# Float32 loads of q, k and V on SP's queue, with the casts moved onto the engines, in an attention and router kernel

## The chip, the cores and the metric

The kernel runs on one core of one Trainium2 chip. The metric is the device time of one execution in microseconds (us). The kernel before has a median of 495.98 us in three runs (494.5 to 497.27).

## What is computed

Two stages follow each other. The first is attention in chunks, for 4 batches, 8 heads, 768 positions and a head size of 64, with inputs in float32. Each chunk of 32 queries sees 16 positions to its left, its own 32, 8 to its right, and 8 memory rows of its head:

```python
for c in range(nc):                       # 24 chunks of 32
    l_start = max(0, c * 32 - 16)
    r_end = min(S, c * 32 + 32 + 8)
    k_full = np.concatenate([mem_k, k[:, :, l_start:r_end]], axis=2)
    v_full = np.concatenate([mem_v, v[:, :, l_start:r_end]], axis=2)
    scores = scale * np.matmul(q_c, k_full.transpose(0, 1, 3, 2))
    a = softmax(scores)
    out[:, :, c_start:c_end] = np.matmul(a, v_full)
```

Its output, 3072 tokens of 512 numbers, goes into a mixture of 8 experts with noisy top-2 routing: `noisy = x @ w_gate + log1p(exp(x @ w_noise)) * noise`. The two best experts of a token compute `relu(x @ w1[e]) @ w2[e]`, and the two results are added with softmax weights.

## The kernel before, in words

**Attention.** Head h and head h+4 are worked on together, in partitions 0 to 63 and 64 to 127; four such pairs make a batch, and the kernel counts 16 pairs n in all. For a pair, `qkT(n)` transposes q and k on PE (L328, L334) and copies them out of PSUM into `qT` (ACT, L330) and `kT` (DVE, L337). `kT` holds 24 windows of 64 columns each: 56 context columns, and 8 memory columns that POOL copies in from `mkT` (L338). `scores(n)` is 48 matmuls of 64 columns (L347), a maximum and a subtraction on DVE (L352, L354), and the exponential on ACT (L355). `probT(n)` transposes the probabilities (PE L362, ACT copy L364). `mix(n)` multiplies them with the windows of V (PE L379), divides by the sum that comes out as column 64 (DVE L383, L384) and writes a tile `xrow` for the batch.

**Loads.** `load_qk(b)` (L249) and `load_v(b)` (L268) are DMAs on POOL's queue that read float32 and write bf16. They read rows of 64 numbers, 256 bytes each: 12,288 rows for q and k of a batch and 10,752 for its V. V is laid out as windows, so that most positions are read twice. The memory rows of V go first into `mv_nat` (L302) and from there into the windows on SP's queue (L271). POOL then multiplies the first and last window by a mask (L274). q and k have two buffers, so batch b+2 is loaded when batch b is done, and so are the two window tiles `vwin0` and `vwin1`.

**Router.** `dispatch(b)` takes a batch's `xrow`, transposes it (L129), copies (L131, DVE and ACT in turn), computes the logits, picks the two experts with some forty small DVE instructions, counts ranks with PE (L169 to L191), and scatters the 6 x 128 rows with indirect DMAs of POOL (L223) into a DRAM table `x_by_pair`, one bucket of 128 rows for each of the 28 pairs of experts, and a spill area behind them. Before that, `fill_blank` writes empty rows to the whole table on SP's queue (L85).

**Experts.** After attention, SP reads the spill rows (L470) and bucket after bucket (L433); eight experts follow (PE L495, L530), their weights cast to bf16 by DMAs on POOL's queue (L420, L421), two experts ahead. A loop at the end (L554) handles spill rows past the first 32; it has no iteration on these inputs.

**Order.** Each engine runs its own instructions in order. The program's order is set by the loop below, and a scheduler moves instructions that do not depend on each other. Tiles come from pools; the pools of the experts are laid over the space that attention's pool `apool` gives back, so what lies on it waits for the end of attention.

```python
for n in range(NPAIR):
    if n + 2 < NPAIR: qkT(n + 2)
    probT(n)
    if n + 1 < NPAIR: scores(n + 1)
    mix(n)
    if n == 0: fill_blank()
    if hp == HP - 1 and b + 2 < B: load_qk(b + 2); load_v(b + 2)
    if hp == 0 and b > 0: dispatch(b - 1, xrows[b - 1])
dispatch(B - 1, xrows[B - 1])
```

Of the kernel before, what the change touches and what calls it, by code (L numbers as in the profile page):

```python
# [12 lines left out]
F32 = mybir.dt.float32  # L13
BF16 = mybir.dt.bfloat16
F32R = mybir.dt.float32r
AX = mybir.AxisListType.X
Alu = mybir.AluOpType
# [4 lines left out]
def kernel(  # L22
# [14 lines left out]
    nc = tc.nc  # L37
    B, H, S, D = q.shape
    n_mem = mem_k.shape[2]
    chunk, left_ctx, right_ctx = 32, 16, 8  # L40
    ncnk = S // chunk
# [13 lines left out]

    identb = const.tile([128, 128], BF16)
# [10 lines left out]
    NROW = NB * CAP + N + 128  # L67
# [13 lines left out]
    def fill_blank():  # L81
        blank = rcon.tile([128, ROW], I32, name="blank")
        nc.vector.memset(blank, 0)
        nc.vector.memset(blank[:, XC:XC + 1].bitcast(F32), float(PAD_TOK))
        nc.sync.dma_start(  # L85
            out=xd.rearrange("(g p) r -> p g r", p=128),
            in_=blank.rearrange("p (o r) -> p o r", o=1).to_broadcast([128, NROW // 128, ROW]),
        )
# [28 lines left out]
    n_spill_i = rcon.tile([128, 1], I32, name="n_spill_i")  # L117

# [3 lines left out]
    def dispatch(b, xrow):  # L122
# [3 lines left out]
        for t in range(BT):  # L126
            p_x = psT.tile([128, KP, 128], BF16, name="p_x", tag="tr")
            for kp in range(KP):
                nc.tensor.transpose(out=p_x[:, kp, :], in_=xrow[:, t, kp * 64:(kp + 1) * 64].bitcast(BF16), identity=identb)  # L129
            xt = rpool.tile([128, KP, 128], BF16, name="xt")  # L130
            (nc.scalar.copy if t % 2 else nc.vector.tensor_copy)(xt, p_x)  # L131
            for kp in range(KP):
                nc.tensor.matmul(out=ps_l[:, t, :], lhsT=xt[:, kp, :], rhs=wgn[:, kp, :], start=(kp == 0), stop=(kp == KP - 1))
# [92 lines left out]
        if b == B - 1:  # L226
            nc.tensor.matmul(out=ps_o[:, BT:BT + 1], lhsT=ones, rhs=seen_ov, start=True, stop=True, skip_group_check=True)
            nc.vector.tensor_scalar(out=n_spill_i, in0=ps_o[:, BT:BT + 1], scalar1=float(SPILL), scalar2=None, op0=Alu.max)
# [4 lines left out]
    psS = actx.enter_context(tc.psum_pool(name="psS", bufs=3))  # L233
    psT = actx.enter_context(tc.psum_pool(name="psT", bufs=2))
# [9 lines left out]
    def load_qk(b):  # L244
        qn = apool.tile([128, HP, BT, 2, D], BF16, name="qn")
        kn = apool.tile([128, HP, BT, 2, D], BF16, name="kn")
        for dst, src in ((qn, q), (kn, k)):
            for hh in range(2):
                nc.gpsimd.dma_start(out=dst[:, :, :, hh, :].rearrange("p h t d -> p (h t) d"),  # L249
                                    in_=src[b, HP * hh:HP * hh + HP].rearrange("h (t p) d -> p (h t) d", p=128))  # L250
        return qn, kn

    def load_v(b):
        vw = vwins[b % 2]
        for hh in range(2):
            p0 = 64 * hh
            o0 = v[b, HP * hh, 0].offset - left_ctx * D
            dst = vw[p0:p0 + WIN, :, :, 0:D].rearrange("p h c d -> p (h c) d")
            src = lambda c, n, j=0, nj=WIN: bass.AP(v.tensor, o0 + (c * chunk + j) * D, [[D, nj], [chunk * D, n], [1, D]])
            nch = HP * ncnk  # L260
            lo, hi = 0, nch
            if b == 0 and hh == 0:
                nc.gpsimd.dma_start(out=dst[left_ctx:, 0:1, :], in_=src(0, 1, left_ctx, WIN - left_ctx))
                lo = 1
            if b == B - 1 and hh == 1:
                nc.gpsimd.dma_start(out=dst[:WIN - right_ctx, nch - 1:nch, :], in_=src(nch - 1, 1, 0, WIN - right_ctx))
                hi = nch - 1
            nc.gpsimd.dma_start(out=dst[:, lo:hi, :], in_=src(lo, hi - lo))  # L268
            for hp in range(HP):
                h = HP * hh + hp  # L270
                nc.sync.dma_start(out=vw[p0 + WIN:p0 + CTX, hp, :, 0:D],  # L271
                                  in_=mv_nat[b * n_mem:(b + 1) * n_mem, h:h + 1, :].to_broadcast([n_mem, ncnk, D]))
        for c, col in ((0, live[:, 0:1]), (ncnk - 1, live[:, 1:2])):
            nc.gpsimd.tensor_scalar(out=vw[:, :, c, 0:D], in0=vw[:, :, c, 0:D], scalar1=col, scalar2=None, op0=Alu.mult)  # L274
# [15 lines left out]
    vwins = []  # L290
    for i in range(2):
        vw = const.tile([128, HP, ncnk, VW], BF16, name=f"vwin{i}")
        nc.gpsimd.memset(vw[:, :, 0, :], 0.0)
        nc.gpsimd.memset(vw[:, :, ncnk - 1, :], 0.0)
        vwins.append(vw)
    mk_nat = const.tile([B * n_mem, HP, 2, D], BF16, name="mk_nat")
    mv_nat = const.tile([B * n_mem, H, D], BF16, name="mv_nat")
    qk = {0: load_qk(0)}
    for b in range(B):
        for hh in range(2):  # L300
            nc.gpsimd.dma_start(out=mk_nat[b * n_mem:(b + 1) * n_mem, :, hh, :], in_=mem_k[b, HP * hh:HP * hh + HP].rearrange("h m d -> m h d"))
        nc.gpsimd.dma_start(out=mv_nat[b * n_mem:(b + 1) * n_mem], in_=mem_v[b].rearrange("h m d -> m h d"))  # L302

# [4 lines left out]

# [5 lines left out]
    p_m = psT.tile([128, HP, B * n_mem], BF16, name="p_m", tag="tr")  # L314
    for hp in range(HP):
        nc.tensor.transpose(out=p_m[:, hp, :], in_=mk_nat[:, hp, :, :], identity=identb[:B * n_mem, :B * n_mem])  # L316
# [5 lines left out]

    def qkT(n):
        b, hp = divmod(n, HP)
        qn, kn = qk[b]
        p_q = psT.tile([128, S], BF16, name="p_q", tag="tr")
        for t in range(BT):
            nc.tensor.transpose(out=p_q[:, t * 128:(t + 1) * 128], in_=qn[:, hp, t, :, :], identity=identb)  # L328
        qT = apool.tile([128, S], BF16, name="qT", bufs=3)
        nc.scalar.copy(qT, p_q)  # L330
        p_k = psT.tile([128, PADL + S + PADR], BF16, name="p_k", tag="tr")
        spots = [(0, 0), (BT - 1, PADL + S + PADR - 128)] + [(t, PADL + t * 128) for t in range(BT)]
        for t, o in spots:
            nc.tensor.transpose(out=p_k[:, o:o + 128], in_=kn[:, hp, t, :, :], identity=identb)  # L334
        kT = apool.tile([128, ncnk, CTX], BF16, name="kT", bufs=3)
        win = bass.AP(p_k.tensor, p_k.offset, [p_k.ap[0], [chunk, ncnk], [1, WIN]])
        nc.vector.tensor_copy(kT[:, :, :WIN], win)  # L337
        nc.gpsimd.tensor_copy(kT[:, :, WIN:], mkT[:, hp:hp + 1, b * n_mem:(b + 1) * n_mem].to_broadcast([128, ncnk, n_mem]))  # L338
        st[n].update(qT=qT, kT=kT)

    def scores(n):
        qT, kT = st[n]["qT"], st[n]["kT"]
        ps = [psS.tile([128, BT, CTX], F32, name="ps_s") for _ in range(2)]
        for c in range(ncnk):
            u, r = divmod(c, 4)
            for hh in range(2):
                nc.tensor.matmul(out=ps[hh][32 * r:32 * r + 32, u, :], lhsT=qT[64 * hh:64 * hh + 64, chunk * c:chunk * (c + 1)],  # L347
                                 rhs=kT[64 * hh:64 * hh + 64, c, :], start=True, stop=True)
        P = apool.tile([128, BT, 2, CTX], BF16, name="P")
        for hh in range(2):  # L350
            mx = apool.tile([128, BT], F32, name="mx", bufs=4)
            nc.vector.tensor_reduce(out=mx, in_=ps[hh], axis=AX, op=Alu.max)  # L352
            sd = apool.tile([128, BT, CTX], F32, name="sd", bufs=4)
            nc.vector.tensor_tensor(out=sd, in0=ps[hh], in1=mx.rearrange("p (u o) -> p u o", o=1).to_broadcast([128, BT, CTX]), op=Alu.subtract)  # L354
            nc.scalar.activation(out=P[:, :, hh, :], in_=sd, func=Act.Exp, scale=scale)  # L355
        st[n]["P"] = P

    def probT(n):
        P = st[n]["P"]
        p_p = psT.tile([128, BT, 128], BF16, name="p_p", tag="tr")  # L360
        for u in range(BT):
            nc.tensor.transpose(out=p_p[:, u, :], in_=P[:, u, :, :], identity=identb)  # L362
        PT = apool.tile([128, BT, 128], BF16, name="PT")
        nc.scalar.copy(PT, p_p)  # L364
        st[n]["PT"] = PT
# [187 lines left out]
    end = nc.values_load(n_spill_i[0:1, 0:1], min_val=SPILL, max_val=N)  # L553
    with tc.For_i(SPILL, end, 128) as i:  # L554
        xl = ld.tile([128, ROW], I32, name="xl")
        nc.sync.dma_start(out=xl, in_=xd[bass.ds(i + NB * CAP, 128), :])
# [3 lines left out]
        nc.vector.tensor_copy(lt, xl[:, XC:XC + 1].bitcast(F32))  # L560
# [7 lines left out]
        for e in range(E):  # L568
# [12 lines left out]
            in_=o, in_offset=None, bounds_check=N - 1, oob_is_err=False)  # L581

# [29 lines left out]
```

## Time and profile before

| what | number |
|---|---|
| median of the three runs | 495.98 us |
| the profiled execution's own time | 495.14 us |
| its span, which all times in the trace count from | 493.4 us |
| busy: PE, DVE, POOL, ACT | 300.5, 166.4, 140.9, 117.2 us |
| first scores L347, first mix L379 | 80.85, 85.77 us |
| last mix done (end of L384) | 218.33 us |
| first spill rows on PE (L476), first expert matmul (L495) | 243.71, 251.36 us |

The page's second part cuts the span into 40 slices of 12.3 us and gives busy shares in tenths; the list of waits says which engine stood idle at which line until what; the timeline gives a start, a duration, the engine, the line, and the idle time ahead in brackets with what ended it. The windows view gives, for a stretch of time, busy time and count of instructions by engine, the granted PE clock, the mean share of the DMA engines, and the GB/s that landed.

### The profile page before, as it was taken

Reading aid. Unit: us, or ns where it says so; the run is one execution under the profiler, and the core shown is the slowest. Engines: PE = TensorE matmul, PEld = TensorE weight load, DVE = VectorE, ACT = ScalarE, POOL = GpSimd, SP = SyncE. Lnnn points to the kernel's source line nnn. Section 1 sums busy time; section 2 is a strip of 40 time slices with the busy share of each in tenths; the row PEclk is TensorE's granted clock in tenths of the full one; section 3 lists DMA queues with packets and bytes.
Section 4 is the critical chain, followed back from the end, with each engine's and each line's share of the span. In section 5 each row is a group of like instructions: output and inputs, shape, how many; then the busy total and the mean of one; then the engine's idle time right before and its main releaser. Section 6 shows DMA issues by size and latency. Waiting matters only on the chain. (4 is left out here: it accounts for less than half of the span.)

```text
span 493.4 us, 8944 instructions
## 1 busy us (share of the span) xinstructions
PE 300.5 (61%) x3745; PEld 179.0 (36%) x3761; DVE 166.4 (34%) x474; ACT 117.2 (24%) x189; POOL 140.9 (29%) x220
## 2 busy tenths in 40 slices
PE   0002103475536246441089779689998999999991
PEld 0002102354425244320045345355554545454540
DVE  1000103474826836825032122221423433333341
ACT  1001001244316135313013213123231223130300
POOL 9007063253185350041320110110213040313132
PEclk9999999999997566555569979979999999999997
DMA  8999999999959951010332453545654665761111
GB/s 199 278 223 66 99 75 130 131 153 162 122 87 141 109 108 29 2 67 0 98 84 43 85 111 63 97 87 85 132 98 106 96 152 86 156 106 73 38 72 66
DMA packets 137531, 50.72 MB, mean 103 GB/s; under 512 B 112487, under 2 KB 131079, under 8 KB 137488
## 3 DMA queue, kind: packets, MB, share of 16 engines
q0 software_dynamic: 115872, 38.21, 97.2%
q1 hardware_dynamic: 21616, 11.91, 10.8%
q8 instruction: 31, 0.51, 0.4%
q14 instruction: 12, 0.10, 0.1%
HBM read 61.23 MB, written 17.81 MB: 160 GB/s over the span
## 5 line engine op out<-in xcount | busy, mean ns | idle before, releaser
L495 PE MATMUL ps_h<-xTb,w1t 128*128 128x384 bf16 (+4 forms) x832 | 111.9, 290 | 1.0 <-DVE xTb L437 1.0
L530 PE MATMUL ps_y<-w2t,ht 128*128 128x512 bf16 x432 | 97.0, 379 | 0.9
L495 PEld LDWEIGHTS <-w1t 128*128 128x128 bf16 x832 | 61.7, 99 | 44.0 <-issue 3.5
L499 ACT ACTIVATE ht<-ps_h 128x512 bf16<-128x512 f32 x64 | 38.2, 597 | 123.8 <-PE ps_h L495 123.8
L530 PEld LDWEIGHTS <-ht 128*128 128x128 bf16 x448 | 43.3, 98 | 51.3
L501 DVE TENSOR_SCALAR ht<-ps_h 128x416 bf16<-128x416 f32 x64 | 37.9, 591 | 64.6 <-PE ps_h L495 64.6
L537 POOL DMA_INDIRECT out_dram<-acc,tid x28 | 27.9, 997 | 78.5 <-DVE acc L536 41.7
L347 PE MATMUL ps_s<-kT,qT 64*32 64x64 bf16 x768 | 12.7, 231 | 59.3 <-POOL kT L338 54.6
L536 DVE SCALAR_TENSOR_TENSOR acc<-ps_y,meta,acc 128x512 f32<-128x512 f32 x28 | 21.0, 751 | 54.5 <-PE ps_y L530 54.5
L223 POOL DMA_INDIRECT x_by_pair<-xrow,slot_i x24 | 24.1, 1002 | 48.5 <-issue 23.8
L534 ACT ACTIVATE acc<-ps_y,meta 128x512 f32<-128x512 f32 x28 | 19.2, 687 | 61.3 <-PE ps_y L530 61.3
L352 DVE TENSOR_REDUCE mx<-ps_s 128x6 f32<-128x384 f32 x32 | 16.6, 551 | 47.3 <-PE ps_s L347 46.0
L347 PEld LDWEIGHTS <-qT 64*32 64x32 bf16 x768 | 8.9, 107 | 63.4 <-issue 59.9
L355 ACT ACTIVATE P<-sd 128x384 bf16<-128x384 f32 x32 | 16.0, 522 | 54.4 <-DVE sd L354 54.4
L316 PE MATMUL p_m<-identb,mk_nat 32*128 32x32 bf16 x4 | 0.3, 182 | 44.9 <-DMA mk_nat<-in_mem_k_dram 44.9
L330 ACT COPY qT<-p_q 128x768 bf16<-128x768 bf16 x16 | 12.7, 794 | 52.8 <-PE p_q L328 52.8
L268 POOL DMA_DIRECT2D vwin<-in_v_dram x8 | 17.9, 2238 | 20.4 <-issue 7.1
L436 PE MATMUL p_t<-identb,xl 128*128 128x128 bf16 x112 | 12.8, 246 | 16.5 <-DMA xl<-x_by_pair 9.6
L364 ACT COPY PT<-p_p 128x768 bf16<-128x768 bf16 x16 | 12.7, 798 | 36.5 <-PE p_p L362 36.4
L420 POOL DMA_DIRECT2D w1t<-in_moe_w_dram x8 | 6.3, 790 | 52.0 <-PE ps_h L495 52.0
L437 DVE COPY xTb<-p_t 128x512 bf16<-128x512 bf16 x28 | 11.9, 424 | 21.2 <-PE p_t L436 20.8
L129 PE MATMUL p_x<-identb,xrow 128*128 128x128 bf16 x96 | 13.7, 291 | 8.4 <-DVE xrow L384 5.6
(129 smaller groups left out, 328.9 us busy)
## 6 DMA issues: line engine op xcount, KB each, us to landing
w1t<-in_moe_w_dram POOLq DMA_DIRECT2D x8, 1024.0 KB
w2t<-in_moe_w_dram POOLq DMA_DIRECT2D x8, 1024.0 KB
x_by_pair<-blank SPq DMA_DIRECT2D x1, 6996.0 KB
vwin<-in_v_dram POOLq DMA_DIRECT2D x6, 672.0 KB
xl<-x_by_pair SPq DMA_DIRECT2D x28, 132.0 KB
qn<-in_q_dram POOLq DMA_DIRECT2D x8, 384.0 KB
kn<-in_k_dram POOLq DMA_DIRECT2D x8, 384.0 KB
vwin<-in_v_dram POOLq DMA_DIRECT2D x2, 665.0 KB
```

The lines of the kernel that those rows point to most:

```text
L223: nc.gpsimd.indirect_dma_start(out=xd_tile[t0 + t], out_offset=bass.IndirectOffsetOnAxis(ap=slot_i[:, t:t + 1], axis=0), in_=xrow[:, t, :] ...
L268: nc.gpsimd.dma_start(out=dst[:, lo:hi, :], in_=src(lo, hi - lo))
L347: nc.tensor.matmul(out=ps[hh][32 * r:32 * r + 32, u, :], lhsT=qT[64 * hh:64 * hh + 64, chunk * c:chunk * (c + 1)], rhs=kT[64 * hh:64 * hh ...
L352: nc.vector.tensor_reduce(out=mx, in_=ps[hh], axis=AX, op=Alu.max)
L355: nc.scalar.activation(out=P[:, :, hh, :], in_=sd, func=Act.Exp, scale=scale)
L495: nc.tensor.matmul(out=ps_h[:, off:off + n], lhsT=w1t[:, kp, f * 128:(f + 1) * 128], rhs=rhs(kp), start=(kp == 0 and i == 0), stop=(kp == ...
L499: nc.scalar.activation(out=ht[:, f, lo:hi], in_=ps_h[:, :hi - lo], func=Act.Relu)
L501: nc.vector.tensor_scalar(out=ht[:, f, lo:hi], in0=ps_h[:, :hi - lo], scalar1=0.0, scalar2=None, op0=Alu.max)
L530: nc.tensor.matmul(out=ps_y, lhsT=ht[:, f, j * CAP:(j + 1) * CAP], rhs=w2t[:, f, :], start=(f == 0), stop=(f == FB - 1))
L534: nc.scalar.activation(out=acc[p], in_=ps_y, func=Act.Copy, scale=gate)
L536: nc.vector.scalar_tensor_tensor(out=acc[p], in0=ps_y, scalar=gate, in1=acc[p], op0=Alu.mult, op1=Alu.add)
L537: nc.gpsimd.indirect_dma_start(out=out_tile[p], out_offset=bass.IndirectOffsetOnAxis(ap=tid[p][:, 0:1], axis=0), in_=acc[p], in_offset=Non ...
```

## The change

q and k are loaded as float32 on SP's queue, the first batch in pieces of one pair. PE transposes them as float32 with a float32 identity, three to a PSUM tile, and ACT alone copies them out in four pieces of 384 columns as bf16. `kT` is one row of 16 + 768 + 8 columns, whose two edges POOL fills; each chunk's context is a slice of it, and the memory columns have matmuls of their own. V and its memory rows are loaded as float32 on SP's queue into tiles `vf` of half a batch, and POOL casts each half into the window tile. The memory keys come on ACT's queue. The copy of the probabilities goes from ACT to DVE, the router's copies all go to ACT. PSUM is divided otherwise: the scores have one buffer for each half instead of three shared, the transposes three instead of two. `fill_blank` writes 3,616 rows instead of 6,784, so the loop at the end, which has no iteration, gathers its rows.

```diff
+    ident = const.tile([128, 128], F32)
+    make_identity(nc, ident)
-    NROW = NB * CAP + N + 128
+    NROW = NB * CAP + N
+    BLK = NB * CAP // SPILL + 1
...
-        blank = rcon.tile([128, ROW], I32, name="blank")
+        blank = rcon.tile([BLK, ROW], I32, name="blank")
...
-            (nc.scalar.copy if t % 2 else nc.vector.tensor_copy)(xt, p_x)
+            nc.scalar.copy(xt, p_x)
...
-    psS = actx.enter_context(tc.psum_pool(name="psS", bufs=3))
-    psT = actx.enter_context(tc.psum_pool(name="psT", bufs=2))
+    psS = actx.enter_context(tc.psum_pool(name="psS", bufs=1))
+    psT = actx.enter_context(tc.psum_pool(name="psT", bufs=3))
...
-    def load_qk(b):
-        qn = apool.tile([128, HP, BT, 2, D], BF16, name="qn")
-        kn = apool.tile([128, HP, BT, 2, D], BF16, name="kn")
+    def load_qk(b, fine=False):
+        qn = apool.tile([128, HP, BT, 2, D], F32, name="qn")
+        kn = apool.tile([128, HP, BT, 2, D], F32, name="kn")
+        step = 1 if fine else HP
+        for h0 in range(0, HP, step):
+            for dst, src in ((qn, q), (kn, k)):
+                for hh in range(2):
+                    nc.sync.dma_start(out=dst[:, h0:h0 + step, :, hh, :].rearrange("p h t d -> p (h t) d"),
...
+        for g in range(2):
+            vf = apool.tile([128, HV, ncnk, D], F32, name="vf")
+            for hh in range(2):
...
+                nc.sync.dma_start(out=dst[:, lo:hi, :], in_=src(lo, hi - lo))
+                for i in range(HV):
+                    nc.sync.dma_start(out=vf[p0 + WIN:p0 + CTX, i], in_=mem_v[b, h0 + i].rearrange("m (o d) -> m o d", o=1).to_broadcast([n_mem, ncnk, D]))
+            nc.gpsimd.tensor_copy(vw[:, HV * g:HV * g + HV, :, 0:D], vf)
...
+        kT = apool.tile([128, PADL + S + PADR], BF16, name="kT", bufs=3)
+        for src, dst, o in ((qn, qT, 0), (kn, kT, PADL)):
+            for g in range(2):
+                p_t = psT.tile([128, HT * 128], F32, name="p_t", tag="tr")
+                for t in range(HT):
+                    nc.tensor.transpose(out=p_t[:, t * 128:(t + 1) * 128], in_=src[:, hp, g * HT + t, :, :], identity=ident)
+                nc.scalar.copy(dst[:, o + g * HT * 128:o + (g + 1) * HT * 128], p_t)
+        nc.gpsimd.tensor_copy(kT[:, :PADL], kT[:, PADL:2 * PADL])
+        nc.gpsimd.tensor_copy(kT[:, PADL + S:], kT[:, S + PADL - PADR:S + PADL])
...
+                nc.tensor.matmul(out=ps[hh][32 * r:32 * r + 32, u, :WIN], lhsT=qT[hs, chunk * c:chunk * (c + 1)],
+                                 rhs=kT[hs, chunk * c:chunk * c + WIN], start=True, stop=True)
...
+                nc.tensor.matmul(out=ps[hh][32 * r:32 * r + 32, u, WIN:], lhsT=qT[hs, chunk * c:chunk * (c + 1)],
+                                 rhs=mkT[hs, hp, b * n_mem:(b + 1) * n_mem], start=True, stop=True)
...
-        nc.scalar.copy(PT, p_p)
+        nc.vector.tensor_copy(PT, p_p)
```

## The prediction

> **What bounds the kernel now.** I read the page's slices first, then the list of waits, then the timeline around the longest waits, then windows for rates. The page's queue lines say who moves the data, and the waits who suffers:
>
> ```profile
> q0 software_dynamic: 115872, 38.21, 97.2%
> q1 hardware_dynamic: 21616, 11.91, 10.8%
> ```
>
> POOL's queue (q0) carries almost everything. Attention stands still for it:
>
> ```profile
> PE ps_s L347 <- POOL kT L338: 54.6, 4, 29.5
> PE p_m L316 <- DMA mk_nat<-in_mem_k_dram: 44.9, 1, 44.9
> POOL vwin L274 <- DMA vwin<-in_v_dram: 30.7, 2, 17.5
> ```
>
> PE has nothing until 44.9 us, then waits 54.6 us at four places for `kT`. The copy L338 that it waits for is short; it is queued on POOL behind V's landing:
>
> ```profile
> 66.24 1.84 POOL L274 TENSOR_SCALAR vwin<-vwin,live 128x256 bf16<-128x256 bf16 x2 [17.52 <-DMA vwin<-in_v_dram]
> ...
> 80.44 0.93 POOL L338 COPY kT<-mkT 128x192 bf16<-128x192 bf16 x3
> 80.85 0.92 PE L347 MATMUL ps_s<-kT,qT 64*32 64x64 bf16 x72 [29.50 <-POOL kT L338]
> ```
>
> The later two long waits look alike. Here POOL's scatters and the mask stand ahead of the copy:
>
> ```profile
> 139.10 1.85 POOL L274 TENSOR_SCALAR vwin<-vwin,live 128x256 bf16<-128x256 bf16 x2 [1.16 <-issue]
> 141.11 1.03 POOL L223 DMA_INDIRECT x_by_pair<-xrow,slot_i  x1 [0.17 <-issue]
> 142.45 1.00 POOL L223 DMA_INDIRECT x_by_pair<-xrow,slot_i  x1 [0.30 <-issue]
> 143.45 0.64 POOL L338 COPY kT<-mkT 128x192 bf16<-128x192 bf16 x2
> 143.86 0.31 PE L347 MATMUL ps_s<-kT,qT 64*32 64x64 bf16 x16 [11.76 <-POOL kT L338]
> ```
>
> The first mix of each batch (L379) starts at 85.8, 109.8, 150.2 and 188.6 us and attention ends at 218.3: cycles of 24.0, 40.4, 38.4 and 29.7 us. In the second, 40.4 - 11.8 of that wait = 28.6 us is work. The end is a chain: last mix, router, scatters, reading back, experts.
>
> ```profile
> 217.31 1.02 DVE L384 TENSOR_TENSOR xrow<-ps_o,rec 128x384 bf16<-128x384 f32 x2
> ...
> 243.71 0.18 PEld L476 LDWEIGHTS <-s_x 32*128 32x128 bf16 x4 [12.47 <-DMA s_x<-x_by_pair]
> ```
>
> Experts begin at 251.36 with PE as their bound, and the edit leaves them alone. So the price is what moves the end of attention, plus what happens between it and the experts.
>
> **Part 1: the start.** The loads go to SP, ahead of the blank (the order of the changed program puts it behind two batches). No row shows 256-byte float32 rows on SP's queue; the nearest are the same rows on POOL's:
>
> ```profile
> 51.00:66.00 15.00, 0.35 (x4) 0.18 (x2) 0.86 (x1) 0.06 (x1) 0.00 (x0) 1.00 3.66 90
> 71.00:79.00 8.00, 0.00 (x0) 0.00 (x0) 0.00 (x0) 0.00 (x0) 4.36 (x3) 1.00 2.82 146
> ```
>
> At 128 landed bytes a row, 146 GB/s (q, k) is 1,140 rows per us, and 90 GB/s (V, windows) is 700. Both queues end on the same transfers from DRAM, so I take these. The other end is the blank's 1,056-byte rows, with 278 GB/s between 12 and 30 us shared with q: about 235 a us. q and k of a batch: 12,288/1,140 = 10.8 us. V with its memory rows, which now come from DRAM, 10,752 + 1,536 = 12,288: /700 = 17.6 us. SP is free at 2.4 us, so V lies at 30.8, plus 1.7 to be seen (L470's issue at 242.02 to PE at 243.71).
>
> Then POOL casts the second half of V and masks. The cast of 128x3072 float32 to bf16 is not in the trace. L338 copies 192 elements in 357 ns, L438 8 in 191 ns: 0.90 ns an element, so 0.19 + 2.77 = 2.95 us. The mask L274 does 256 in 920 ns, 2.87 ns an element: 9.0 us. I take 2.95, since a cast has one operand like the copy; both ends stay. [...]
>
> First mix: 30.8 + 1.7 + 2.95 + 1.84 = 37.3 us instead of 85.8: **-48.5**. qkT and scores of four pairs are done in that wait; it covers them.
>
> **Part 2: the cycles.** PE, for one pair: 14 bf16 transposes go, 12 float32 ones come. Bf16 ones follow each other by 0.10 us (six in 0.82, 0.30 for the last). [...] 12 x 0.2 - 14 x 0.10 = +1.0 us. The 48 extra score matmuls: 48 take 0.61 in the trace, +0.6. Some hides beside DVE; I book +1 a pair, 4 a batch. [...]
>
> DVE for a pair: the kT copy (0.85) goes, a 768-column copy comes, 0.55 between L131's 0.42 for 512 and 0.85 for 1,344; six router copies a batch (half of them 0.42 on DVE) leave. Nearly even: a small gain, not booked. ACT gets four copies of 384 (L355's 0.52 each) for two of 0.80: +0.5 a pair on an engine that is busy 14.5 of 40 us between 110 and 150; nothing. One score buffer per half: the next scores wait for two DVE pairs (2.0 us) and DVE has 2 us of other work meanwhile, so it is bound by DVE as before (4.3 us a pair from 99 to 104); nothing booked.
>
> The new wait is POOL's. In the changed order the casts of the third batch stand behind the scatters of the second, those of the fourth behind the scatters of the third, and the first mix of that batch waits for both: slot list to POOL 1.0, six scatters by 1.3 = 7.8, two casts 5.9, mask 1.84, handover 0.4: 17 us with PE idle, since the scores ahead are done. Behind the casts stand only edge copies of `kT`, needed later. Cycle one has no scatter ahead and its casts (7.7) run beside the router's DVE chain: 28.6 + 4 = 32.6. Cycles two and three: 28.6 + 4 + 17 = 49.6. After the last first-mix only four mixes remain, the scores having moved ahead: four by 1.5 of DVE (L383 0.18, L384 0.55, twice) and a copy, about 2.5 each: 10. Sum 141.8 against 132.5: **+9.3**. DMA for later batches (28.4 us each) fits a cycle.
>
> Attention then ends at 179 us.
>
> **Part 3: after attention.** The blank (3.8 MB for 7.2) lies under part 2: nothing. ACT alone does the router's copies: 6 x 0.59 = 3.5 us against about 4.0 from 218.7 to 222.6, nothing. But float32 tiles make `apool` 95,672 bytes a partition instead of 50,936, and expert weights now lie on it: in the changed order L420 and L421 for two experts, issued from 81 us on before, come after the last mix and before the last six scatters, on the same queue. Four loads of 1.05 MB:
>
> ```profile
> 268.00:274.00 6.00, 6.00 (x30) 2.74 (x28) 0.00 (x0) 2.75 (x4) 0.00 (x0) 1.00 1.01 174
> ```
>
> At 174 GB/s they take 24 us, from 2 to 3 us after the last mix to about 27; the scatters (issued 14 to 22 us after it) land behind them at 28 to 31, and the spill rows are asked for at about 32 instead of 23.7 (242.02 - 218.33). **+8**; 0 if scatters pass the weights, +14 at 118 GB/s (1.05 MB in the 8.9 us of L421's load after 281). The weights themselves are there before the first expert.
>
> **Sum.** 495.14 - 48.5 + 9.3 + 8 = 463.9, **464 us**. That starts from the profiled execution, 0.84 us below the median of the three runs.
>
> **Rivals.**
> A. Better hidden: casts and scatters run while PE still works, since POOL is idle half of a cycle; cycles as before (24, 40, 38), last 10: 112 instead of 141.8, so **434**. For it: each engine is under 60% busy in these windows. Against: the order on POOL.
> B. The cast costs like the mask, 9.0 us: +6 at the start, +8 in cycle one (19.8 of POOL against 12 of cover), +12.1 in each of two others: +38, **502**, slower. Place: POOL ahead of each batch's first mix. It decides against the change from 8.0 us a cast (6.05 us more cost 38; the gain is 31). For it: L274. Against: L338.
> [...]
> D. The change does not do what it says, as SP's queue takes small rows no faster: at 600 rows a us V lies at 43, every batch needs 41 us and DMA is nearly the bound: about **480**; at 235, attention would be DMA alone and far slower, which I give 2%.
>
> **How the numbers follow.** Forecast 0.52 (445 to 485), A 0.17, B 0.14, C 0.12, D 0.05. A measurement of this kernel tells 0.5% (2.5 us) from no change. Faster: 0.52 + 0.17 + 0.03 of D + 0.04 of C = 0.76; same 0.05 of C; slower the rest, 0.19. The range 432 to 503 takes in A, B, C and D's milder half and leaves out a little at both ends.
>
> **What would show it.** Right: the first L379 at 35 to 40 us; POOL casts near 3 us; 128x128 float32 transposes near 0.2 us apart; before the third and fourth batches a PE wait of about 17 us released by POOL's mask; expert weights issued right after the last mix, and spill rows 30 us or more behind it. Wrong: a first mix after 50 us, casts over 6 us, PE busy through the cycles, or scatters that pass the weights.

## The result, and the profile after

The changed kernel takes 675.99 us (670.9 to 676.35) where the kernel before takes 495.24 us in the same series: a ratio of 1.362, with a 95% interval of 1.354 to 1.371. Forecast were 464 us and a range of 432 to 503. The profiled execution has a span of 674.6 us. Where some executions of a kernel were over 1.5% longer than its fastest, the times and ratios below leave them out; the traces of e1_blank32 and e3_blank_full are of such longer executions.

The page's slices show it at a glance. Each column is 16.9 us, and the rows are PE's busy tenths, the mean busy share of the 16 DMA engines in tenths, and GB/s:

```profile
PE   3502552000000000164175040696969999999993
...
DMA  9999940000000002999791159336271746557102
GB/s 166 133 115 191 116 59 22 21 21 21 21 21 21 21 21 65 220 129 176 145 121 19 48 85 215 84 62 111 38 134 32 142 84 127 119 96 152 67 28 87
```

From the eighth to the fifteenth column PE stands almost idle and DMA moves a steady 21 GB/s. The queues have changed places, as the change says (queue, packets, MB, share of 16 engines' time):

```profile
q1 hardware_dynamic: 111267, 32.94, 31.3%
q0 software_dynamic: 15968, 26.32, 19.4%
```

The list of waits has two new entries of the same length, and a third that the prediction expected (engine, tile, line, releaser: us in total, times, longest):

```profile
POOL x_by_pair L227 <- DMA x_by_pair<-blank: 168.7, 1, 168.7
PE p_t L338 <- DMA qn<-in_q_dram: 166.0, 1, 166.0
PE ps_o L390 <- POOL vwin L287: 53.6, 6, 21.9
```

POOL's first scatter waits for the blank; PE waits for q of the third batch. The timeline of SP's queue says what the two have in common:

```profile
88.66 0.80 SPq L88 DMA_DIRECT2D x_by_pair<-blank  x1
89.57 174.02 SPq L256 DMA_DIRECT2D qn<-in_q_dram  x1
```

The load of q stands right behind the blank on the queue, and its issue alone lasts 174 us, about as long as the blank takes to land. The windows of the trace (us, busy time and count by engine, granted clock, DMA share, GB/s) give the rates that the prediction had to guess:

```profile
6.00:16.00 10.00, 4.72 (x49) 4.44 (x50) 0.29 (x1) 3.84 (x7) 0.39 (x2) 1.00 1.30 224
24.00:48.00 24.00, 4.83 (x205) 4.16 (x205) 5.06 (x11) 4.14 (x9) 3.13 (x3) 0.50 1.02 110
95.00:255.00 160.00, 3.87 (x206) 3.13 (x206) 15.42 (x55) 2.83 (x6) 6.94 (x4) 0.50 0.07 22
```

q and k run at 224 GB/s (875 rows of 256 bytes per us), V at 110 (430 rows). The third line is the blank: a DMA share of 0.07 is about that of one engine of 16 (0.0625). Counted in the trace's packets, 101 blank rows land in each 5 us, 20.2 per us, so 3,616 rows take 179 us.

Where the time went, from the trace of before, of after, and of a later run with the blank mended (e5_blank128):

| stage | before | forecast | after | e5_blank128 |
|---|---|---|---|---|
| first mix | 85.8 | 37.3 | 56.1 | 57.0 |
| cycle 1, 2, 3 | 24.1, 40.4, 38.4 | 32.6, 49.6, 49.6 | 51.9, 226.3, 52.2 | 51.3, 62.5, 54.1 |
| last cycle | 29.7 | 10 | 8.1 | 8.1 |
| end of attention to the request for spill rows | 23.7 | 31.7 | 27.4 | 27.4 |
| from there to the end | 251.4 | 251.4 | 252.6 | 252.0 |
| span | 493.4 | 462 | 674.6 | 512.3 |

The blank's stall is in one cell: 226.3 against 62.5, **164 us**. The rest of the miss, some 50 us of span, is in the first mix and the cycles, and has other causes.

### The profile page after: what moved, and what is told of

It reads as the page before. It is cut to its first block, busy times and chain, and to the rows that moved or that the text cites. A ratio compares the mean times of both kernels' runs of the same rounds, so it can differ in the third digit from the quotient of the medians.

```text
span 674.6 us, 10496 instructions
## 1 busy us (share of the span) xinstructions
PE 319.0 (47%) x4497; PEld 194.8 (29%) x4497; DVE 162.0 (24%) x464; ACT 126.7 (19%) x233; POOL 115.5 (17%) x207
## 4 chain that ended last, share of the span: by engine, by line
PE 37%; SPq 31%; DMA 9%; issue 9%; DVE 5%; POOL 5%; ACT 2%; another core or an unknown queue 0%; POOLq 0%; DVEq 0%; ACTq 0%
SPq L256 26%; PE ps_h L506 14%; PE ps_y L541 13%; DMA kn<-in_k_dram 5%; SPq L284 4%; PE p_t L338 4%; DMA xl<-x_by_pair 3%; POOL vwin L285 2%; POOL x_by_pair L227 2%; PE p_t L447 1%; PE ps_o L390 1%; DMA qn<-in_q_dram 1%; PE p_p L373 1%; DMA x_by_pair<-xrow,slot_i 1%; DVE mx L363 1%
## 5 line engine op out<-in xcount | busy, mean ns | idle before, releaser
L338 PE MATMUL p_t<-ident,qn 128*128 128x128 f32 x96 | 22.6, 385 | 166.0 <-DMA qn<-in_q_dram 166.0
L338 PEld LDWEIGHTS p_t<-ident,qn 128*128 128x128 f32 x96 | 15.8, 197 | 166.8 <-issue 166.1
L339 ACT CAST qT<-p_t 128x384 bf16<-128x384 f32 x32 | 15.2, 478 | 246.2 <-PE p_t L338 245.9
L390 PE MATMUL ps_o<-vwin,PT 64*32 64x65 bf16 x768 | 12.7, 228 | 64.2 <-POOL vwin L287 53.6
L390 PEld LDWEIGHTS <-PT 64*32 64x32 bf16 x768 | 9.3, 107 | 67.6 <-issue 59.8
L338 PE MATMUL p_t<-ident,kn 128*128 128x128 f32 x96 | 19.5, 359 | 14.1 <-DMA kn<-in_k_dram 14.1
L285 POOL CAST vwin<-vf 128x3072 bf16<-128x3072 f32 x8 | 21.8, 2748 | 22.4 <-DMA vf<-in_mem_v_dram 22.4
L352 PE MATMUL ps_s<-kT,qT 64*32 64x56 bf16 x768 | 12.6, 207 | 19.7 <-DVE c L154 11.9
L363 DVE TENSOR_REDUCE mx<-ps_s 128x6 f32<-128x384 f32 x32 | 16.8, 552 | 19.8 <-PE ps_s L358 19.6
L135 ACT COPY xt<-p_x 128x512 bf16<-128x512 bf16 x24 | 13.0, 586 | 37.7 <-PE p_x L133 34.3
```

Source lines behind the costliest of these rows:

```text
L285: nc.gpsimd.tensor_copy(vw[:, HV * g:HV * g + HV, :, 0:D], vf)
L338: nc.tensor.transpose(out=p_t[:, t * 128:(t + 1) * 128], in_=src[:, hp, g * HT + t, :, :], identity=ident)
L390: nc.tensor.matmul(out=po[hh][32 * r:32 * r + 32, u, :], lhsT=PT[64 * hh:64 * hh + 64, u, 32 * r:32 * r + 32], rhs=vw[64 * hh:64 * hh + 64 ...
```

## The experiments

Times are compared by their ratio to the kernel before in the same series, since its median went from 487 to 496 us from series to series. The edits are printed in short form. From e7_mem_long on, a run without "before" in its name has e5_blank128's blank too.

**The blank's shape.** Four runs with one question: why does it run on one engine?

e1_blank32: the same rows from 32 partitions.

```
-  xd[:NB*CAP+SPILL, :].rearrange("(p g) r -> p g r", p=113)   # blank [113, 32, ROW]
+  xd[:NB*CAP+SPILL, :].rearrange("(p g) r -> p g r", p=32)    # blank [32, 113, ROW]
```

> The changed kernel with one edit: the same 3,616 blank rows are written from 32 partitions with 113 rows each instead of 113 partitions with 32 each. Theory S (spread): the DMA engines that a transfer uses follow from the size of its outermost dimension; 113 is prime, so the whole blank ran on one engine at 20.2 rows per us (101 rows in each 5 us of the trace), 179 us, and the loads behind it on SP's queue and the scatters that need it waited. 32 is spread over 16 engines: the blank takes 11 to 13 us, PE's wait of 166 us for qn goes, the first mix of the third batch is bound by V's loads and POOL (about 155 us), the fourth's comes 52 us later, and the end 288 us behind that: 485 to 500 us. Rival Q (queue): SP's queue is jammed by the float32 loads in flight and the blank is only the transfer that happens to be in it; the shape changes nothing: 660 to 680 us. Rival W (DRAM writes): writing the table while the loads read is what is slow; same bytes, so again 660 to 680 us.

Measured: 509.0 and 513.6 us, ratio 1.049 (1.040 to 1.059). The wait of 166 us is gone. The blank's window:

```profile
91.00:104.00 13.00, 4.17 (x159) 3.49 (x160) 10.34 (x22) 5.80 (x11) 7.66 (x6) 0.50 0.91 203
```

A share of 0.91 instead of 0.07. Theory S holds against Q and W; the time is 9 to 14 us above its range, and the blank took 19.5 us, not 12.

e2_blank4: the same with `p=4` and 904 rows each.

> The changed kernel with the blank written from 4 partitions with 904 rows each: 4 engines by theory S, 904 rows on each at 20.2 per us = 45 us, some 32 us longer than with 16 engines. The loads of the third batch are behind it on those four engines, so the time is 20 to 35 us above that of e1_blank32, about 515 us, and the stretch of 1,056-byte rows lasts 45 us at about 81 rows per us. Rivals Q and W: 660 to 680 us as the changed kernel.

Measured: 652.82 us, ratio 1.340. Far from 515:

```profile
100.00:220.00 120.00, 3.87 (x206) 3.13 (x206) 10.60 (x53) 2.19 (x5) 2.12 (x3) 0.50 0.21 25
```

The share is near that of four engines, yet they move hardly more than one did: a row takes 144 ns on its engine instead of 52. So the number of engines is only half of the rule; where the rows are read from limits too.

e3_blank_full: the blank of the kernel before (6,784 rows, 128 partitions) in the changed kernel.

> The changed kernel with the whole blank of the kernel before: 6,784 rows from 128 partitions, almost twice the bytes of the change. Theory S: 16 engines, 24 us at 285 rows per us, so about 6 us above e1_blank32 and some 170 us below the changed kernel, although it writes more. Rival W: more bytes to write, so slower than the changed kernel, over 700 us. Rival Q: 660 to 680 us.

Measured: 514.4 us, from one execution alone. It writes 1.9 times the bytes and is some 155 us faster than the changed kernel, at 340 GB/s between 92 and 108 us. W is dead.

e4_before_blank113: the kernel before with the 113-partition blank alone.

```
-  blank = rcon.tile([128, ROW]); out=xd.rearrange("(g p) r -> p g r", p=128)
+  blank = rcon.tile([113, ROW]); out=xd[:NB*CAP+SPILL, :].rearrange("(p g) r -> p g r", p=113)
```

> The kernel before with nothing but the 113-partition blank (3,616 rows instead of 6,784), still the first large transfer on SP's queue. Theory S: it takes 179 us there too, from about 6 to 185 us; the memory rows of V stand behind it on the same queue, so the first mix moves from 85.8 to about 188 us, and the time from 495 to about 590 to 600 us. Rivals Q and W: half the bytes and no float32 loads on the queue, so no slower than before, 488 to 496 us.

Measured: 641.18 us, ratio 1.316 (1.306 to 1.326). One edit that halves the bytes costs this kernel nearly a third, so the float32 loads are not needed for it, which Q and W did not expect. It cost some 45 us more than forecast. The longest wait is that for the queue, as expected, since the memory rows of V stand behind the blank:

```profile
POOL vwin L274 <- DMA vwin<-mv_nat: 147.6, 1, 147.6
```

The wait lasted longer than forecast, because the blank did: its rows land from 4.7 to 215.6 us, not to 185. Between 20 and 65 us the trace has 73 of them in each 5 us where the changed kernel has 101, beside 73 to 137 rows of POOL's queue, and the same goes on to 135 us; behind that they land 101 at a time again. So the rows of the two queues land about one for one, as if one engine served both in turn. In that stretch `mk_nat`, on POOL's queue, comes late as well (PE waits for it until 69.8 us instead of 44.9), but this wait ends long before the other and sets nothing here. The rest of the delay lies behind the blank: POOL goes on at 220 us and issues five loads until 234.4, ahead of the copy that PE waits for. The first mix came at 239.7 us instead of the 188 that were expected.

e5_blank128 and e6_blank124 part the two halves of the rule:

```
+  xd[:3584, :].rearrange("(p g) r -> p g r", p=128)   # e5; 32 rows by a second DMA
+  xd[:3596, :].rearrange("(p g) r -> p g r", p=124)   # e6; 20 rows by a second DMA
```

> The changed kernel with the blank written from 128 partitions with 28 rows each, and its last 32 rows by a second DMA from 32 partitions. After e2_blank4 theory S has a second half, P: with 4 source partitions the whole blank ran at 23 rows per us, not at 4 x 20.2, with 32 at 187, and with 128 (e3_blank_full) at 320, so the rate is the smaller of 20.2 rows per us for each engine and a limit by the partitions that are read. 128 partitions on 16 engines give 320 per us, 11.3 us instead of the 19 us of e1_blank32: 5 to 10 us less than that run, 1.03 to 1.04 of the kernel before. If the blank is no longer what waits, no difference to e1_blank32.

> As e5_blank128, but 124 partitions with 29 rows each (and 20 rows by a second DMA). 124 = 4 x 31. Theory S with P: 4 engines, all partitions: 81 rows per us, 44 us, packets of 50 to 55 ns, and the time 25 to 35 us above e5_blank128. P alone (only the source partitions count): 124 partitions are as good as 128, 11 to 12 us and no difference to e5_blank128; but then the 113 of the change should have been good too. Engines that slow each other whatever the source: 23 rows per us as in e2_blank4 and about 650 us.

Measured: e5 509.65 us, ratio 1.041 (1.035 to 1.048); e6 552.67 us, ratio 1.132 (1.125 to 1.139). First e5's window, then e6's:

```profile
92.00:100.00 8.00, 2.34 (x56) 1.71 (x54) 5.96 (x7) 3.87 (x6) 5.46 (x4) 0.50 1.08 341
```

```profile
95.00:140.00 45.00, 3.87 (x206) 3.13 (x206) 13.14 (x55) 2.19 (x5) 4.67 (x4) 0.50 0.25 69
```

128 partitions give 341 GB/s. 124 of them give 69 at a share of 0.25, about four engines of 16, as theory S had it from 124 = 4 x 31. So partitions alone (P) are not the rule: with nearly as many of them as e5, e6 has a fifth of its rate. Nor are engines alone: e2 has as many as e6 and about a third of its rate. That the smaller of the two limits counts fits all the runs only roughly, as e6 reached 65 rows per us, not the 81 of four engines; why is not shown. Whether e5 is faster than e1 is not resolved, as their intervals overlap.

Over these runs the share goes with the outermost dimension: 0.07 at 113, about one engine of 16; 0.21 at 4 and 0.25 at 124, about four; 0.91 at 32 and 1.08 at 128, about sixteen. For these five that number is the largest up to 16 that divides the dimension; no other was run. For the other half, the partitions that are read, e2 (4) moved 25 GB/s, e1 (32) 203 and e5 (128) 341; what in the hardware sets these rates is not shown.

**V's rate.** e7_mem_long fills the memory rows' places with long runs:

```
-  dma(vf[p0+56:p0+64, i], mem_v[b, h0+i] broadcast 24 times)           # 192 rows of 256 bytes
+  dma(vf[p0+56:p0+64, i], AP(v, [[24*D, 8], [1, 24*D]]))               # 8 runs of 6,144 bytes
```

> As e5_blank128, but the memory rows of V are not loaded: each of their places is filled with the same number of bytes of V instead, 8 runs of 6,144 bytes for each head in place of 192 rows of 256 (so the attention is that of other memory values). V of the first batch took 36 us from the first issue (17.0) to the second cast (53.0), 430 rows per us instead of the 700 that the prediction took. Theory P (bytes into few partitions): 8 partitions take about as little as the 4 of e2_blank4 gave, so the memory rows cost as much in long runs: first cast at 36 to 38 us, no difference over 5 us to e5_blank128. Theory R (rows): the memory rows are 12.5% of V's rows but on 8 engines; in long runs they cost nothing: first cast at 25 to 30 us, the time 20 to 40 us less. Theory W (the windows themselves run at 430 to 500 rows per us as float32): first cast at 33 to 35, 8 to 15 us less.

Measured: 503.5 us, ratio 1.031 (1.025 to 1.037); casts at 35.4 and 49.6 instead of 37.6 and 53.2. The first cast lies between the forecasts of P and W, and the time fell by 6 us, a little under W's. The memory rows are a small part; the windows themselves are slow.

e9_v0_two_queues puts half of the first V on ACT's queue, e10_v_two_queues half of every V on POOL's:

```
+  eng = nc.scalar if b == 0 and hh == 1 else nc.sync     # e9
+  eng = nc.gpsimd if hh == 1 else nc.sync                # e10, windows only
```

> As e5_blank128, but for the first batch the half of V that goes to partitions 64 to 127 is issued on ACT's queue, beside the other half (partitions 0 to 63) on SP's. In e5_blank128, V's rows ran at 430 per us and q and k, on all 128 partitions, at 860 with the same 256 bytes. Theory P (a row costs at the place it is written to, and the 56 partitions of a window reach half as many places as 128): two halves side by side run at twice the rate, V of the first batch has landed at about 34 us instead of 52, the first mix comes at 38 to 42 instead of 57, and the time falls by 10 to 17 us, to about 495 (1.01 of the kernel before). Theory E (32 ns a row on its engine, whatever the partition): the same engines carry the same rows, V has landed at 50 to 53 as before and the time stays within 3 us of e5_blank128.

> As e5_blank128, but for every batch the windows for partitions 64 to 127 go by POOL's queue (float32, no cast), the others stay on SP's. Theory P: V of a batch takes about 15 us instead of 29, q and k 14: the transfers no longer bound the cycles, the first mix comes at about 40, and the order on POOL (scatters ahead of casts, 15 us of waits for the third and the fourth batch) bounds what is left: 465 to 480 us, 0.95 to 0.98 of the kernel before. Theory E: no faster than e5_blank128, 505 us or more.

Measured: e9 509.11 us, 1.028 (1.025 to 1.032); e10 519.67 us, 1.048 (1.044 to 1.051). By the times theory E holds, and the first mixes came at 59.7 and 54.1 us, not at 40. But neither run tests what it was meant to. In e9 ACT's half ran beside q and k and was issued by 33 us, while SP's half was issued from 24 us on, behind q and k: they were hardly side by side. In e10 POOL's half came in packets of 4,096 bytes, the middle half of them of 375 to 520 ns each, q and k of the first batch beside them fell to some 220 rows per us, and PE began at 21.6 us instead of 10.5.

e13_v_rows128 and e14_v_dense56 change destination and source apart:

```
+  dma(vf on 128 partitions, AP(v, [[D, 128], [128*D, 48], [1, D]]))              # e13, one DMA for half a batch
+  dma(vf[p0:p0+56],         AP(v, [[D, 56], [56*D, 48], [1, D]]))                # e14
```

> As e5_blank128, but each half of a batch's V is filled by one DMA of 6,144 rows of 256 bytes to all 128 partitions, with the source pattern of q and k (so the attention is that of other values, and the memory rows of V are left out). Same number of rows, bytes, queue and order. If the 56 (and 8) partitions written at a time set the 430 rows per us, or the source's pattern of windows does: 860 rows per us as q and k, both casts done by about 35 us instead of 56, the first mix at 36 to 40, 480 to 495 us in all. If float32 V on this queue is slow for another reason (its tile, its place in the order): no change, 505 to 515 us.

> As e5_blank128, but the windows are filled from rows that lie densely (window c from row 56 c on instead of 32 c, no row read twice; so the attention is that of other values). Destination, 56 partitions at a time, row size and count stay. If the destination sets the rate: still 430 rows per us, casts at 37 and 53, 505 to 515 us. If the source's pattern (8 KB from window to window, rows read twice) sets it: 750 to 860 rows per us, the second cast at about 36 to 40 and 480 to 495 us.

Measured: e13 475.84 us, 0.959 (0.953 to 0.966); e14 510.01 us, 1.028 (1.023 to 1.033). V in e13, then in e14:

```profile
21.00:29.00 8.00, 3.79 (x169) 3.07 (x167) 3.07 (x6) 3.05 (x7) 0.78 (x4) 1.00 0.98 195
```

```profile
24.00:48.00 24.00, 4.82 (x204) 4.17 (x205) 5.64 (x12) 4.37 (x10) 3.13 (x3) 0.51 0.95 110
```

Another source with the same 56 partitions stays at 110 GB/s to the last digit; 128 partitions at a time give 195 in this window and some 225 in the best 5 us, counted by packets. So in these runs the destination sets the rate. In e13 the packets are also longer (1,024 bytes, 82 ns, which is 20.5 for each 256); but q and k, in packets of 256 bytes to 128 partitions, reach 224 GB/s beside the 110 of the same packets to 56, so the partitions explain it without the packets' length. Why 56 partitions take about half of the 224 GB/s of 128 is not shown.

**What is left beside the blank and V's rate.** e8_v_pool loads V as the kernel before does, e11_v_pool_late_weights ties the first expert weights to the last V, e16_v_first also ties q of the second batch to V of the first:

```
+  load_v of the kernel before                                          # e8
+  if e < 2: copy(w1t[:, 0, 0:1], vwins[1][:, 0, 5, 0:1]), same w2t     # e11, ahead of the weights' DMAs
+  if b == 1: copy(qn[:, 0, 0, 0, 0:1], vwins[0][:, 0, 5, 0:1])         # e16, ahead of q's DMAs
```

> As e5_blank128, but V is loaded as in the kernel before: windows by POOL's queue, cast to bf16 by the DMA, and memory rows from the small tile on SP's queue; no casts on POOL. Everything else of the change (float32 q and k on SP, float32 transposes, slices of kT, copies, buffers) stays. Theory V (what is left of the loss beside the blank is V on SP's queue with its casts): the first mix at 27 to 38 us, cycles of 30 to 42 us, attention's end at 140 to 165 us, 425 to 455 us in all, 0.88 to 0.93 of the kernel before. Rival T (the float32 transposes, 96 extra matmuls of a pair and the single score buffers make the cycles long): the first mix is as early, but cycles stay at 45 to 55 us: 475 to 500 us.

> As e8_v_pool, but the weights of the first two experts are issued only when V of the last batch lies (a copy of one column ties them to it). In e8_v_pool they came at 50 to 85 us, 4 MB among the loads of the second batch, and PE waited 28.9 us for kn at 91.5. Theory C (these weights held up k): the wait for kn falls to below 8 us, attention ends at 185 to 200 us instead of 219, 460 to 478 us in all, 0.94 to 0.98 of the kernel before. Rival D (the loads of q, k and V together are the bound and the weights only filled a gap): kn still comes after 80 us and the time stays at 485 to 495 us.

> As e11_v_pool_late_weights, but q of the second batch is asked for only when V of the first lies (a copy of one column ties it). If V of the first batch is late because q and k of the second share the engines with it: V lies at 28 to 32 us instead of 42, the first mix at 32 to 40 instead of 55, 462 to 475 us. If V's windows have a limit of their own on POOL's queue: V lies at 40 or later, q and k of the second batch come later for nothing, 480 to 495 us.

Measured: e8 492.82 us, 1.009 (1.006 to 1.012); e11 481.19 us, 0.973 (0.969 to 0.977); e16 479.49 us, 0.969 (0.964 to 0.974). The wait for k in e8, then in e11:

```profile
PE p_t L341 <- DMA kn<-in_k_dram: 35.9, 4, 28.9
```

```profile
PE p_t L341 <- DMA kn<-in_k_dram: 11.8, 2, 8.8
```

e8's time lies in the range of rival T and far above V's, but T's long cycles are not there: the third takes 33.0 us. In e8 the expert weights no longer wait for attention's end: they are fetched at 50 to 85 us, among the loads of the second batch. Theory C named that cause, and e11 bears it out; the ratio lies where it was expected, the time 3 us above, and the longest wait for k is 0.8 us above. e16 moved the first mix only from 54.6 us to 52.6. Its tying copy, which waits for V, ran at 37.5 us, between the two forecasts, and the mask stood behind another issue on POOL until 41.8. So q and k of the second batch were not what held V; until 32 us the trace has rows of the first batch's q and k beside it.

e15_casts_act takes V off POOL:

```
-  nc.gpsimd.tensor_copy(vw..., vf);  nc.gpsimd.tensor_scalar(vw..., live)
+  nc.scalar.copy(vw..., vf);         nc.vector.tensor_scalar(vw..., live)
```

> As e5_blank128, but the casts of V run on ACT and the masks on DVE, so that nothing of V stands behind scatters on POOL. Theory O (the order on POOL is what the third and fourth batch wait for, as the prediction said, 15 us each): both waits of PE for V fall below 5 us, 480 to 490 us, 0.96 to 0.99 of the kernel before. Rival L (V lands no earlier, and the wait only changes its name): PE waits 10 us or more at the same place for ACT or a DMA, the time falls by less than 8 us.

Measured: 494.25 us, 0.996 (0.994 to 0.999). First e5_blank128 at its third batch, then e15:

```profile
163.25 0.97 POOL L228 DMA_INDIRECT x_by_pair<-xrow,slot_i  x1 [0.30 <-issue]
164.22 5.44 POOL L286 CAST vwin<-vf 128x3072 bf16<-128x3072 f32 x2
...
170.73 0.59 PE L391 MATMUL ps_o<-vwin,PT 64*32 64x65 bf16 x46 [15.34 <-POOL vwin L288]
```

```profile
151.91 5.39 ACT L286 CAST vwin<-vf 128x3072 bf16<-128x3072 f32 x2
157.72 0.59 PE L391 MATMUL ps_o<-vwin,PT 64*32 64x65 bf16 x46 [2.54 <-DVE vwin L288]
...
166.21 0.99 PE L391 MATMUL ps_o<-vwin,PT 64*32 64x65 bf16 x48 [7.34 <-DVE xrow L396]
```

V lay by 152 us and was held by the scatters: theory O by the waits (2.5 and 2.7 us are left), though the time stays 4 us above its range. Half of each wait comes back at the next pair, as PE then waits 7.3 us for DVE, which is in the router. By the spans 16 us went, by the ratios 4.3% or some 21, against two waits of 15.4.

e17_best adds two moves to e16: memory rows of the first V on ACT's queue, edges of `kT` on DVE.

> As e16_v_first, but the memory rows of the first batch's V go by ACT's queue and the two edge copies of kT run on DVE. If the queue positions are what V of the first batch waits for: V lies at about 33 us (10,752 window rows at some 460 per us from 9 us on), PE's wait of 17.7 us for kT's edges goes, the first mix comes at 35 to 40 us instead of 52.6, and 462 to 472 us in all, 0.93 to 0.955 of the kernel before. If the windows themselves lie at 40 us or later, the first mix stays behind 44 us and the time at 474 to 482 us.

Measured: 482.6 to 488.8 us, 0.981 (0.974 to 0.987), against e16's 0.969 (0.964 to 0.974). V's windows lay at 42 us, so the last sentence applies: the first mix came at 45.0 us, though the time is above what it says. The move to ACT has a price of its own:

```profile
14.73 16.76 ACTq L281 DMA_DIRECT2D vwin<-mv_nat  x8
```

Eight issues hold ACT for 16.8 us, and PE stands for 15.3 us behind the copy of `kT`. This is not what lost the time, though, as the first mix still came 7.6 us before e16's. The loss is in the first two cycles (53.0 and 59.9 us for 42.0 and 50.7), and no run takes them apart.

e12_before_blank128 is the kernel before with the smaller blank in e5's shape:

> The kernel before with nothing but the smaller blank, written from 128 partitions (3,584 rows, and 32 by a second DMA): the part of the change that writes less, without its 113 partitions. The blank shares the engines with q and k of the first batch there, until 30 us, and 3.3 MB less at 280 GB/s is 12 us: the first scores and everything behind them come up to 10 us earlier, 485 to 490 us (0.98 to 0.995). If the start is bound by POOL's queue alone, no difference.

Measured: 484.66 us, 0.977 (0.974 to 0.980). The first mix comes at 74.4 instead of 85.8, and the 132.7 us from there to the end of attention are the 132.6 of before. So the part of the change that writes less was worth 11 us in itself, in another shape. e11, e12, e16 and e17 beat both kernels, e16 and e11 by most; which of these two is faster is not resolved, as their intervals overlap. (e13 is left out here, since it loads other values.)

## Why the prediction was wrong

**The step that failed**: "The blank (3.8 MB for 7.2) lies under part 2: nothing." The blank was priced at nothing, for its bytes had halved. The only rate that the prediction has for it, 278 GB/s shared with q, is that of before, where its outermost dimension is 128 (second and third of 40 columns of 12.3 us):

```profile
GB/s 199 278 223 66 99 75 130 131 153 162 122 87 141 109 108 29 2 67 0 98 84 43 85 111 63 97 87 85 132 98 106 96 152 86 156 106 73 38 72 66
```

The diff made that 113, which is prime. At a DMA share of 0.07, about one engine of 16, its 3.8 MB took 179 us, on the queue that q of the third batch needs next, and ahead of every scatter: 164 us of the second cycle. Every other error is small beside it, and no rival held it. Rival D had a slow SP queue, but from small rows; for the rest of the miss it came nearest. What in the profile and the diff should have raised the question: the changed dimension, and that the only measured rate belonged to the old one.

**The start, -48.5**: -29.7, and a first mix after 50 us is one of the prediction's own signs of being wrong. q and k were somewhat slow (875 rows per us for 1,140, some 3 us). V was mis-sized: 700 rows per us for the windows against 430, some 11 us; that rate had been measured on another queue, where a row lands as 128 bytes. The second cast began at 52.3 us. The cast (2.95 forecast, 2.74 measured) and the mask (1.84) were right: rival B is dead.

**The cycles, +9.3**: +43.4 with the blank mended. V's rate is in these too: a batch needs 14 us for q and k and 29 for V, 43 where the prediction had 28.4. But SP's queue does not bound a cycle alone: in e5 the loads of V of the second and third batch are all issued by 89.4 and 142.3 us, and the first mixes of these batches come at 108.3 and 170.7; e15, with the same queue, casts the third batch's V at 151.9. e13 takes 16.7 us off the start and 19.6 off the cycles. Only the first is V's rate alone, since e13 also has another order on POOL, with the casts of the third batch ahead of the scatters:

```profile
128.03 2.75 POOL L268 CAST vwin<-vf 128x3072 bf16<-128x3072 f32 x1
130.87 1.83 POOL L270 TENSOR_SCALAR vwin<-vwin,live 128x256 bf16<-128x256 bf16 x2
...
146.77 1.06 POOL L228 DMA_INDIRECT x_by_pair<-xrow,slot_i  x1 [14.07 <-DVE slot_i L205]
```

In the changed kernel the 17 us of PE wait from POOL's order came as 15.4, twice, with the releaser that was named:

```profile
326.84 0.98 POOL L227 DMA_INDIRECT x_by_pair<-xrow,slot_i  x1 [0.30 <-issue]
327.82 5.44 POOL L285 CAST vwin<-vf 128x3072 bf16<-128x3072 f32 x2
...
334.34 0.59 PE L390 MATMUL ps_o<-vwin,PT 64*32 64x65 bf16 x46 [15.38 <-POOL vwin L287]
```

Its price as a term was too high: e15 shows that a third to a half of it comes back as another wait. Rival A (better hidden) is dead.

**Float32 transposes**, 0.2 us each: no run shows the 0.2 of the sum, which was the author's estimate; the changed kernel's trace shows 0.14 to 0.26 each. Six take 0.85 to 0.88 us where the granted clock is 1.00 (15 to 20 us) and 1.54 where it is about half (22 to 26 us); six bf16 ones (L373) take 0.50 at 20.5 us and 0.85 at 26.2. (From 11.8 to 15 us six take 1.36 to 1.54 too. The windows view has a clock of 1.00 there, but the trace's first record of the clock is at 15.5 us.) Both times stand in the timeline:

```profile
17.38 0.88 PE L338 MATMUL p_t<-ident,qn 128*128 128x128 f32 x6
...
59.03 1.54 PE L338 MATMUL p_t<-ident,qn 128*128 128x128 f32 x6
```

**The last cycle, 10**: 8.1. **After attention, +8**: +3.7. The order was as forecast, weights ahead of the scatters, and the scatters did land behind them: the packets of the weights land from 397.0 to 419.0 us, those of the scatters from 418.3 to 421.1. But the four loads ran at some 190 GB/s, not 174, so the spill rows could be asked for 27.4 us after attention, not 31.7:

```profile
395.40 0.87 POOL L431 DMA_DIRECT2D w1t<-in_moe_w_dram  x1 [0.17 <-PE p_x L133]
...
415.20 0.98 POOL L227 DMA_INDIRECT x_by_pair<-xrow,slot_i  x1 [0.31 <-issue]
422.03 0.33 SPq L481 DMA_DIRECT2D s_x<-x_by_pair  x1
```

With the blank mended and V at 128 partitions' rate, e13 comes to 476.2 us of span against the 462 that the sum stands for. That is not the sum come true: e13's first and last cycles are 9 us longer each than forecast, its third is 5 shorter without the wait for POOL, and the way to the spill rows is 4.5 shorter. What stays open is the rest of e5's and e13's cycles (42.0, 50.8, 44.8 and 18.7 in e13), which no run takes apart further.

## What to carry to other kernels

Read a DMA's price from its shape before its bytes: in these runs the share of the 16 engines went with its outermost dimension (0.07, about one engine, at 113; 1.08 at 128). The blank at 0.07 held what stood behind it on its queue (174 us), and in e4 rows of another queue landed only about one for one with its own. A rate carried over from the trace holds for the partitions and the queue it was measured on (224 GB/s for q and k to 128 partitions, 110 for V to 56); where the change alters these, it is a bound, and the range must reach to it.

## What the runs showed of the hardware

- A queue's issue can be the longest bar of a timeline: 174.02 us for one load behind the blank in the changed kernel, 16.76 us for eight small ones on ACT in e17_best, where ACT computes nothing for 16.41 us.
- The granted clock fell to 0.50 while PE was nearly idle (3.87 us busy from 95 to 255 us). What sets the clock stays open. The view prints 1.00 also where the trace has no record of the clock (up to 15.5 us in the changed kernel, 148 in the kernel before, 402 in e4), so such a 1.00 says nothing.
